# Second layer's first products as seven products of quarters for two column groups by two token halves

## The chip, the core and the metric

One core of one Trainium2 chip runs the whole program. The metric is the device time of one execution in microseconds (us). TensorE (PE) multiplies, ScalarE (ACT), VectorE (DVE) and GpSimd (POOL) do the elementwise work, and SyncE (SP) issues nearly all transfers.

## What is computed

A thresholded attention gives 2304 tokens of 512 numbers; a gated layer and a second layer follow. The change is in the second layer alone (fp32 throughout, d_model 512, d_ff 2048):

```python
x = _moe_ref(x=x, **moe_kwargs)          # gate, val, out: 512 -> 1536 -> 512
return _moe2_ref(x=x, **moe2_kwargs)
...
def _moe2_ref(x, w_in, w_out):
    h = x @ w_in                          # 2304 x 2048, "the first products"
    g = np.where(h >= 1, h, np.where(h <= -1, 0.0, (h + 1) ** 2 / 4))
    return g @ w_out                      # 2304 x 512
```

## The kernel before

Every fp32 product is made of three fp32r matmuls: both factors are split into a high part (an ACT copy that rounds) and a low part (a DVE subtraction), and high·high, high·low and low·high are added up in PSUM. The attention runs first (about 0 to 300 us), then the gated layer (called layer 0, to 747.5 us), then the second layer. Tokens go in three passes of 768 (`T`), each in two halves of 384 (`HT`); d_ff goes in column groups of 128 (`f`), 12 in layer 0 and 16 in the second. x lies transposed, so that a matmul has 128 columns of weights as its stationary side and 384 tokens as its moving side.

`order` lists the steps: layer, pass, column group. One step of the second layer is a call of `hidden` (L497): for each half, `up` (L466) makes 4 blocks of 128 of the contraction by 3 matmuls of 384 (L472 to L474, into a PSUM tile `pu`); then DVE clamps (L522), ACT squares (L525), DVE takes the maximum with h (L526), ACT rounds it to `hh` (L529) and DVE leaves the rest in `hl` (L531). Between these stand the splits of the next group's weights (`split_parts`, L183 and L185: `ih`, `il` for the first products, `oh`, `ol` for the second) and, in the last step of a pass, the splits of the next pass's x (`split_xs`, L462 and L464). Behind the step, PE gets the second products of the step before it (`down`, L546): 6 blocks of 128 tokens by 3 matmuls of 512 (L563, into PSUM tiles `w`), which add up over a pass. After a pass `finish` (L568) moves its six blocks out of PSUM, in turn on DVE (L586) and ACT (L588), and sends them off. Layer 0 is alike; its `finish` writes `xall`, the x of the second layer, with pieces of 512 and 256 (L573, L575).

So PE's order in the second layer is: 24 matmuls of 384, 18 of 512, and so on, 48 times. Each engine works in the order in which the program wrote its instructions; an instruction that waits holds all behind it. PE has two PSUM banks of first products (`a0`, `a1`) and three double ones of second products.

Of the kernel before, what the change touches and what calls it, by code (L numbers as in the profile page):

```python
# [29 lines left out]
def kernel(  # L30
# [17 lines left out]
    nc = tc.nc  # L48
# [21 lines left out]
    raw = ctx.enter_context(pool("raw", 2))  # L70
    zero = ctx.enter_context(pool("zero", 1, space=DRAM))
    scratch = ctx.enter_context(pool("scratch", 1, space=DRAM))
    ws0 = ctx.enter_context(pool("ws0", 1))
# [9 lines left out]
    rbs = [const.tile([P, S], F32, name=f"rb_{i}") for i in range(2)]  # L83
# [6 lines left out]
    xflat = const.tile([P, 2 * KD * T], F32R, name="xflat")  # L90

# [19 lines left out]
    def load_w(ph, g):  # L111

        f, i = divmod(g, 3 - ph)
        ins, wo = ((w_gate, w_val), w_out) if ph == 0 else ((w2_in,), w2_out)
        if i < len(ins):
            src = ins[i][:, 2 * f * P : 2 * (f + 1) * P].rearrange("(k p) f -> p k f", p=P)
        else:
            src = wo[f * P : (f + 1) * P, :].rearrange("p (k f) -> p k f", k=KD)
        early = ph == 0 and g < 6
        t = (raw if early else pools["words"]).tile([P, 2 * KD * P], F32, tag="raw", name="raw")  # L120
# [44 lines left out]
    def split_list(ph, t, f, whole=True):  # L165

        ni = 2 - ph
        m = len(wsp_n)
        wsp_n.append(f)
        a, b = (ws0 if m % x == 0 else pools[y] for x, y in ((2, "ws"), (3, "wo")))  # L170
        ih = a.tile([P, 2, KD, P], F32R, tag="ih", name="ih")
        il = a.tile([P, 2, KD, P], F32R, tag="il", name="il")
        oh = b.tile([P, DM], F32R, tag="oh", name="oh")
        ol = b.tile([P, DM], F32R, tag="ol", name="ol")
# [12 lines left out]

        return [part(*x) for x in at]
# [4 lines left out]
    def attention():  # L193
# [141 lines left out]
        def spread(p):  # L335
            dr = drs.pop(p)
            for a, n, o in ((nf * P, nf * P, 0), (R, R, 2 * nf * P)):
                src = bass.AP(tensor=dr.tensor, offset=dr.offset + o, ap=[[a, 2], [0, D], [1, n]])
                nc.sync.dma_start(out=rbs[p % 2][:, (o > 0) * nf * P :][:, :n], in_=src)

        def normalise(p, s):
            x, c = x_of(p), slice(s * HS, s * HS + HS)
            nc.gpsimd.tensor_tensor(x[:, c], x[:, c], rbs[p % 2][:, c], op=ALU.mult)
# [105 lines left out]
    def ffn(att):  # L449


        with ExitStack() as st:
            sb = lambda n, b, **kw: st.enter_context(pool(n, b, reuse_waits="tile", **kw))
# [43 lines left out]
            def hidden(ph, t, f, nxt, work):  # L497


                hh = hs.tile([P, T], F32R, tag="hh", name="hh")  # L500
                hl_ = hs.tile([P, T], F32R, tag="hl", name="hl")
                sp = split_parts(*nxt) if nxt and nxt not in wsp else iter(())
                xs = iter(())
                for n in range(2):
                    c = slice(n * HT, n * HT + HT)
                    act = hp_.tile([P, HT], F32, tag="act", name="act")
                    if ph == 0:
                        if (s := (ph, t, f, n)) in early:
                            pg, pv = early.pop(s)
                            nc.scalar.activation(act, pg, AF.Sigmoid)  # L510
                        else:
                            pg, pv = (ps_a.tile([P, 512], F32, tag=f"a{i}", name="pgv")[:, :HT] for i in range(2))
                            up(0, t, f, n, 0, pg)
                            nc.scalar.activation(act, pg, AF.Sigmoid)  # L514
                            up(0, t, f, n, 1, pv)
                        if n == 0:
                            run(itertools.islice(sp, 1))
                        nc.vector.tensor_tensor(act, pv, act, op=ALU.mult)  # L518
                    else:
                        pu = ps_a.tile([P, 512], F32, tag=f"a{n}", name="pu")[:, :HT]  # L520
                        up(1, t, f, n, 0, pu)
                        nc.vector.tensor_scalar(act, pu, -1.0, 1.0, op0=ALU.max, op1=ALU.min)  # L522
                        if n == 1:
                            run(itertools.islice(xs, 4))
                        nc.scalar.activation(act, act, AF.Square, scale=0.5, bias=half)  # L525
                        nc.vector.tensor_tensor(act, pu, act, op=ALU.max)  # L526
                        if n == 1:
                            run(itertools.islice(xs, 4))
# [9 lines left out]
                hts[ph, t, f] = (hh, hl_)  # L538
# [7 lines left out]
            def down(ph, t, f, y, blocks=range(T // P)):  # L546
                hh, hl_ = hts[ph, t, f]
                oh, ol = wsp[ph, t, f][2:]
                first, last = f == 0, f == NF[ph] - 1
                if ph == 0:  # L550
                    for a, b, d in spans:
                        ds_, c = slice(d * P, d * P + P), slice(a - d * T, b - d * T)
                        new = first and a % 512 == 0
                        for m, (l, r) in enumerate(((oh, hh), (oh, hl_), (ol, hh))):
                            nc.tensor.matmul(  # L555
                                at(y, a, b), l[:, ds_], r[:, c], start=new and m == 0, stop=last and m == 2,
                                skip_group_check=True,
                            )
                    return
                for i in blocks:  # L560
                    ts_ = slice(i * P, i * P + P)
                    for m, (l, r) in enumerate(((hh, oh), (hl_, oh), (hh, ol))):
                        nc.tensor.matmul(  # L563
                            y[i % 3][:, i // 3], l[:, ts_], r,
                            start=first and m == 0, stop=last and m == 2,
                        )
# [24 lines left out]
            order = [(ph, t, f) for ph in range(2) for t in range(NPASS) for f in range(NF[ph])]  # L591
# [13 lines left out]
            early, taken = {}, []  # L605
# [3 lines left out]
            for step, free in att:  # L609
# [4 lines left out]
                if free:  # L614
                    pools["words"] = sb("words", 6)
# [3 lines left out]
                    pools["ws"] = sb("ws", 1)  # L619
                    pools["wo"] = sb("wo", 2)  # L620
                    hp_ = sb("hp_", 2)
# [11 lines left out]
            hs = sb("hs", 2, side="right")  # L633
            ps_a = sb("ps_a", 1, space=PSUM)
            for i in range(2):
                highs[i] = kp.tile([P, 3 * KD * P], F32, name=f"high_{i}")
            ring[:0] = [kp.tile([P, 3 * KD * P], F32, name=f"w32_{i + 2}") for i in range(3)]
            w2s = [kp.tile([P, 2 * KD * P], F32, name=f"w2_{i}") for i in range(2)]
# [5 lines left out]
            for s in range(len(order)):  # L644
                nxt = order[s + 1] if s + 1 < len(order) else None
                t = order[s][:2]
                ops = 8 if t == (0, 0) else 5
                if s + 2 < len(order) and order[s + 2][:2] > (0, 0):
                    load_step(*order[s + 2])
                hidden(*order[s], nxt, itertools.islice(conv, ops))  # L650
                if s > 0:
                    ph, t, f = order[s - 1]
                    if f == 0:
                        y = [wide() for _ in range(3)]
                    if s < len(order) - 1:
                        down(ph, t, f, y)
                        if f == NF[ph] - 1:
                            finish(ph, t, y)

            for b in (range(3), (3,), (4,), (5,)):  # L660
                down(*order[-2], y, b)
                for i in b:
                    down(*order[-1], y, (i,))
                    finish(ph, t, y, (i,))
# [50 lines left out]
```

## Time and profile before

| | |
|---|---|
| median of 3 runs | 1160.7 us (1160.56 to 1160.76) |
| the profiled execution | 1160.46 us |
| span in its profile | 1158.7 us |
| PE busy | 1131.9 us, 98% of the span, 6516 matmuls |
| DVE busy | 796.9 us, 69% |
| ACT busy | 559.5 us, 48% |
| POOL busy | 137.6 us, 12%, all of it before 310 us |

The span is what the engines' records cover; 1.8 us of the profiled execution lie around it. In the timeline an entry has its start, its length, engine, line and operation, and in brackets how long its engine had been idle before it and what ended that. Busy shares are means over stages; what a change in one stage is worth is read in that stage.

### The profile page before, as it was taken

The numbers are of one execution on the slowest core, as the hardware profiler recorded it, in microseconds if no ns is written. First come the engines' busy times: TensorE is split into PE (matmuls) and PEld (weight loads), VectorE is DVE, ScalarE is ACT, GpSimd is POOL, SyncE is SP. The second block draws the span as 40 slices with busy tenths as digits, with TensorE's granted clock in tenths as the row PEclk, the third lists the DMA queues.
The fourth block names the chain that finished last, engine by engine and source line by source line (L and its number), as shares of the span: only waits on it lengthen the run. The fifth ranks groups of instructions, "written<-read, shape, count | busy, mean of one in ns | idle before, by whom it ended". The sixth has DMA issues, their size and how long they took to land.

```text
span 1158.7 us, 17531 instructions
## 1 busy us (share of the span) xinstructions
PE 1131.9 (98%) x6516; PEld 968.6 (84%) x6516; DVE 796.9 (69%) x1491; ACT 559.5 (48%) x1027; POOL 137.6 (12%) x315
## 2 busy tenths in 40 slices
PE   8999999999899999999999999999999999999998
PEld 5655655556799999999999999999898989989897
DVE  6888888887699998665676662465557555575554
ACT  5777777787344444333343332443435343454333
POOL 3444544554100000000000000000000000000000
PEclk9999999999899999999999999999999999999999
DMA  4323223221645655434434323121211412041201
GB/s 129 87 74 101 69 74 83 67 58 33 244 165 198 208 194 193 162 136 161 168 129 163 136 88 131 37 72 56 63 47 57 145 55 73 19 163 56 72 2 55
DMA packets 59381, 122.33 MB, mean 106 GB/s; under 512 B 8976, under 2 KB 35232, under 8 KB 59296
## 3 DMA queue, kind: packets, MB, share of 16 engines
q1 hardware_dynamic: 59152, 121.20, 32.1%
q8 instruction: 52, 0.85, 0.3%
q14 instruction: 33, 0.27, 0.1%
q10 hardware_dynamic: 144, 0.00, 0.0%
HBM read 98.57 MB, written 22.62 MB: 105 GB/s over the span
## 4 chain that ended last, share of the span: by engine, by line
PE 90%; DVE 6%; issue 2%; ACT 2%; DMA 1%; POOL 0%; DVEq 0%; ACTq 0%; POOLq 0%
PE w L563 17%; PE w L555 13%; PE pgv L472 8%; PE pgv L473 8%; PE pgv L474 8%; PE av L312 6%; PE pu L474 6%; PE pu L473 6%; PE pu L472 6%; PE w L288 5%; PE w L245 5%; DVE s L254 2%; PE w L241 2%; DVE p L274 1%; DVE high L158 1%
## 5 line engine op out<-in xcount | busy, mean ns | idle before, releaser
L472 PE MATMUL pgv<-xflat,ih 128*128 128x384 f32 x560 | 188.6, 337 | 6.0 <-ACT act L514 4.1
L473 PE MATMUL pgv<-xflat,ih 128*128 128x384 f32 x560 | 188.4, 336 | 0.0
L474 PE MATMUL pgv<-xflat,il 128*128 128x384 f32 x560 | 188.2, 336 | 0.0
L529 ACT ACTIVATE hh<-act 128x384 fp32r<-128x384 f32 x168 | 88.5, 527 | 180.8 <-DVE act L518 119.0
L525 ACT ACTIVATE act<-act,half 128x384 f32<-128x384 f32 x96 | 59.2, 617 | 167.7 <-DVE act L522 167.7
L531 DVE TENSOR_TENSOR hl<-act,hh 128x384 fp32r<-128x384 f32 x168 | 93.5, 557 | 62.0 <-ACT hh L529 62.0
L254 DVE TENSOR_SCALAR_CACHE_REDUCE s<-w,nscale 128x576 f32<-128x576 f32 x144 | 112.7, 816 | 33.7 <-PE w L245 23.9
L474 PE MATMUL pu<-xflat,il 128*128 128x384 f32 x384 | 128.9, 336 | 0.0
L473 PE MATMUL pu<-xflat,ih 128*128 128x384 f32 x384 | 128.9, 336 | 0.0
L472 PE MATMUL pu<-xflat,ih 128*128 128x384 f32 x384 | 128.4, 334 | 0.0
L518 DVE TENSOR_TENSOR act<-pgv,act 128x384 f32<-128x384 f32 x70 | 38.9, 555 | 118.9 <-PE pgv L474 115.1
L563 PE MATMUL w<-oh,hh 128*128 128x512 f32 x288 | 113.9, 395 | 0.4 <-DVE xall L586 0.4
L563 PE MATMUL w<-ol,hh 128*128 128x512 f32 x288 | 114.0, 396 | 0.0
L563 PE MATMUL w<-oh,hl 128*128 128x512 f32 x288 | 113.9, 396 | 0.0
L472 PEld LDWEIGHTS pgv<-xflat,ih 128*128 128x128 f32 x560 | 105.9, 189 | 8.4 <-ACT act L514 4.7
L274 DVE SCALAR_TENSOR_TENSOR p<-s,mx,ex 128x576 f32<-128x576 f32 x144 | 112.0, 810 | 0.5 <-POOL lt L281 0.5
L266 ACT ACTIVATE ex<-s,mx 128x576 f32<-128x576 f32 x144 | 104.8, 775 | 7.1 <-DVE s L254 6.7
L473 PEld LDWEIGHTS pgv<-xflat,ih 128*128 128x128 f32 x560 | 105.9, 189 | 1.8 <-DVE xflat L464 0.2
L474 PEld LDWEIGHTS pgv<-xflat,il 128*128 128x128 f32 x560 | 106.0, 189 | 0.0
L526 DVE TENSOR_TENSOR act<-pu,act 128x384 f32<-128x384 f32 x96 | 53.5, 558 | 70.2 <-ACT act L525 70.2
L514 ACT ACTIVATE act<-pgv 128x384 f32<-128x384 f32 x70 | 34.2, 489 | 134.6 <-PE pgv L474 134.4
L288 PEld LDWEIGHTS w<-ident,p 128*128 128x128 f32 x576 | 62.8, 141 | 41.6 <-ACT ex L266 36.6
(82 smaller groups left out, 2184.4 us busy)
## 6 DMA issues: line engine op xcount, KB each, us to landing
w<-saved SPq DMA_DIRECT2D x48, 512.0 KB
w<-saved SPq DMA_DIRECT2D x24, 768.0 KB
raw<-in_moe_w_out_dram SPq DMA_DIRECT2D x28, 512.0 KB
saved<-w SPq DMA_DIRECT2D x12, 768.0 KB
raw<-in_moe_w_in_dram SPq DMA_DIRECT2D x16, 512.0 KB
saved<-w SPq DMA_DIRECT2D x16, 512.0 KB
raw<-in_moe_w_gate_dram SPq DMA_DIRECT2D x12, 512.0 KB
raw<-in_moe_w_val_dram SPq DMA_DIRECT2D x12, 512.0 KB
```

The costliest lines, as they stand in the source:

```text
L254: nc.vector.tensor_scalar(t[:, e], w[:, :, :HS], nscale, None, op0=ALU.mult, op1=ALU.min, accum_out=mx[:, 0, e : e + 1])
L266: nc.scalar.activation(ex[:, e], t[:, e], AF.Exp, scale=-1.0, bias=mx[:, 0, e : e + 1])
L274: nc.vector.scalar_tensor_tensor(pr[:, e], t[:, e].rearrange("p a b -> p (a b)"), mx[:, 1, e : e + 1], ex[:, e].rearrange("p a b -> p (a b ...
L288: nc.tensor.transpose(wt[:, e, cs], pr[:, e, cs], ident)
L312: nc.tensor.matmul(av[e * D : e * D + D, :n], vs[p % 3][:, e, c], rt[r][:, e, c] if c < nf else rl[r], start=c == 0, stop=c == nf,)
L472: nc.tensor.matmul(ps, ih[:, i, kk], xh[:, kk, c], start=(kk == 0), stop=False)
L473: nc.tensor.matmul(ps, ih[:, i, kk], xl[:, kk, c], start=False, stop=False)
L474: nc.tensor.matmul(ps, il[:, i, kk], xh[:, kk, c], start=False, stop=(kk == KD - 1))
L529: nc.scalar.activation(hh[:, c], act, AF.Copy)
L531: nc.vector.tensor_tensor(hl_[:, c], act, f32(hh[:, c]), op=ALU.subtract)
L555: nc.tensor.matmul(at(y, a, b), l[:, ds_], r[:, c], start=new and m == 0, stop=last and m == 2, skip_group_check=True,)
L563: nc.tensor.matmul(y[i % 3][:, i // 3], l[:, ts_], r, start=first and m == 0, stop=last and m == 2,)
```

## The change

Two neighbouring column groups form a pair `q` (8 to a pass, 24 in all). A pair's first products are a 2 by 2 matrix of quarters: two column groups by two token halves, with the contraction of 512 cut in two halves as well. Instead of eight products of quarters, seven are made (P.0 to P.6), each 2 blocks of the contraction by 3 matmuls of 384; their factors are quarters of x and of the weights, or sums and differences of such quarters, and the four results are put together from the seven by additions. POOL makes the factors: `w_sums` four subtractions of 256 columns a pair, `x_sums` four additions of 768 columns a pass. `x_splits` splits seven blocks of 768 columns a pass, `w_splits` 512, 256 and 1024 columns a pair, `out_split` the weights of the second products. Then PE makes the 36 matmuls of 512 of the pair before. The activation works on 768 columns of one group: ReLU and square on ACT, one operation on DVE, the copy `hh` on ACT, `hl` on DVE. There are still two PSUM banks, `ps[0]` and `ps[1]`; P.2 adds to what P.0 left in `ps[0]`. SBUF is laid out anew, with the order of instructions in attention and layer 0 kept on every engine.

```diff
-                    else:
-                        pu = ps_a.tile([P, 512], F32, tag=f"a{n}", name="pu")[:, :HT]
-                        up(1, t, f, n, 0, pu)
-                        nc.vector.tensor_scalar(act, pu, -1.0, 1.0, op0=ALU.max, op1=ALU.min)
...
-                        nc.scalar.activation(act, act, AF.Square, scale=0.5, bias=half)
-                        nc.vector.tensor_tensor(act, pu, act, op=ALU.max)
...
+            PRODUCTS = ((0, 0, 0, 1), (1, 1, 1, 1), (0, 2, 3, 0), (1, 3, 4, 1), (0, 4, 5, 1), (1, 5, 6, 0), (0, 6, 2, 0))
...
+                op = nc.gpsimd.tensor_tensor
+                op(s1, a21, a22, op=ALU.add)
+                op(s2, s1, a11, op=ALU.subtract)
+                op(s4, a12, s2, op=ALU.subtract)
+                op(a21, a11, a21, op=ALU.subtract)
+                xops[t] = (a11, a12, s2, a21, s1, a22, s4)
...
+            def x_splits(t):
+                for i, a in enumerate(xops.pop(t)):
+                    xh, xl = (x.rearrange("p (k t) -> p k t", k=HK) for x in x_block(i))
+                    nc.scalar.activation(xh, a, AF.Copy)
+                    nc.vector.tensor_tensor(xl, a, f32(xh), op=ALU.subtract)
+                    yield
...
+                for o, a, b in ((t1, b12, b11), (t2, b22, t1), (t3, b22, b12), (t4, b21, t2)):
+                    nc.gpsimd.tensor_tensor(o, a, b, op=ALU.subtract)
...
+            def activate(i, c, h):
+
+                r = sqs[:, i]
+                nc.scalar.activation(r, c, AF.Relu, scale=0.5, bias=half)
+                nc.scalar.activation(r, r, AF.Square)
+                yield
+                nc.vector.scalar_tensor_tensor(c, c, 1.0, r, op0=ALU.max, op1=ALU.min)
+                nc.scalar.activation(h[0], c, AF.Copy)
+                yield
+                nc.vector.tensor_tensor(h[1], c, f32(h[0]), op=ALU.subtract)
+                yield
+
+            def pair(q):
...
+                if q + 1 < NPASS * NQ:
+                    w_sums(q + 1)
+                if j == NQ - 2 and t + 1 < NPASS:
+                    x_sums(t + 1)
+                outs = [lambda i=i: out_split(q, i) for i in range(2)]
+                xs = x_rest.pop(t, None) if j == 0 else None
+                product(0, ps)
+                nc.scalar.activation(s1, ps[0], AF.Copy)
+                if xs:
+                    run(itertools.islice(xs, 2))
+                product(1, ps)
+                add(c[0][:, t0], ps[1], s1)
+                if xs:
+                    run(xs)
+                else:
+                    while outs:
+                        outs.pop(0)()
+                product(2, ps)
+                nc.scalar.activation(u2, ps[0], AF.Copy)
+                product(3, ps)
+                add(u3, ps[1], u2)
+                product(4, ps)
+                add(c[1][:, t1], ps[0], u3)
+                product(5, ps)
+                add(c[0][:, t1], ps[1], u2)
+                product(6, ps)
+                add(c[1][:, t0], ps[0], u2)
...
+            def behind(q, outs, acts):
...
+                if j == NQ - 1 and t + 1 < NPASS:
+                    xs = x_splits(t + 1)
+                    do(2)
+                    run(itertools.islice(xs, 2))
+                    do(4)
+                    run(itertools.islice(xs, 2))
+                    run(acts[0])
+                    x_rest[t + 1] = xs
+                    return acts[1:]
+                a, b = acts[-2:]
+                for x in acts[:-2]:
+                    run(x)
+                next(a)
+                do(1)
+                next(a)
+                do(2)
+                run(a)
+                do(3)
+                for o in outs:
+                    o()
+                run(b)
+                return []
...
+            for q in range(NPASS * NQ):
+                outs, acts = pair(q)
...
+                left = behind(q, outs, left + acts)
...
+                if q == 0:
+                    down(*order[-1][1:], y)
+                    finish(0, NPASS - 1, y)
+                else:
...
+                        down_pair(q - 1, y)
+                        if q % NQ == 0:
+                            finish(1, q // NQ - 1, y)
```

Three places show what this makes of the engines' queues. The first is ACT at the end of the second layer's first pass, around the evictions of that pass. `w_118` to `w_123` are the PSUM tiles of the second products, `w_2` to `w_4` and `w_0` in other rows buffers of loaded weights, and what stands in brackets is the engine that a row waits for. Before:

```order
L525 ACTIVATE act<-act,half 128x384 [waits DVE_49,Activation_49]
L529 ACTIVATE hh<-act 128x384 [waits DVE_49]
L588 ACTIVATE xall<-w_122 128x512 [waits PE_49]
L588 ACTIVATE xall<-w_123 128x512 [waits DVE_49]
L588 ACTIVATE xall<-w_121 128x2x256 [waits DVE_49]
L525 ACTIVATE act<-act,half 128x384 [waits DVE_49,Activation_49]
L529 ACTIVATE hh<-act 128x384 [waits DVE_49]
```

Now, behind the first pair of the second pass up to the copy of P.0 in the pair after it (L645, whose input `pu` is the bank that P.2 wants):

```order
L623 ACTIVATE hh<-vals 128x768 [waits DVE_49]
L585 ACTIVATE win_88<-w_0_82 128x256 [waits DMAHW4_49,PE_49]
L585 ACTIVATE win_88<-tsum 128x1024 [waits Pool_49]
L596 ACTIVATE wout_89<-w_2_3098 128x512
L596 ACTIVATE wout_3005<-w_3_3099 128x512
L619 ACTIVATE sqs<-vals,half 128x768
L620 ACTIVATE sqs<-sqs 128x768 [waits Activation_49]
L623 ACTIVATE hh<-vals 128x768 [waits DVE_49]
L746 ACTIVATE xall<-w_119 128x512 [waits PE_49]
L746 ACTIVATE xall<-w_120 128x512 [waits DVE_49]
L746 ACTIVATE xall<-w_118 128x2x256 [waits DVE_49]
L645 ACTIVATE act<-pu 128x384 [waits PE_49]
```

The three evictions (L588, now L746) have moved from behind one step's short activation to behind the weight splits and the second activation of a pair, and the first row that takes a first product out of PSUM stands behind them.

The second place is DVE at the start of a pass, where `pu` is again a first product and `xmore` and `xflat` hold the split x. Before, the x splits stand between a half's activation steps:

```order
L464 TENSOR_TENSOR xflat<-xall,xflat 128x384 [waits Activation_49] x4
L522 TENSOR_SCALAR act<-pu 128x384 [waits PE_49]
L464 TENSOR_TENSOR xflat<-xall,xflat 128x384 [waits Activation_49] x2
L526 TENSOR_TENSOR act<-pu,act 128x384 [waits Activation_49]
L464 TENSOR_TENSOR xflat<-xall,xflat 128x384 [waits Activation_49] x2
L531 TENSOR_TENSOR hl<-act,hh 128x384 [waits Activation_49]
```

Now:

```order
L625 TENSOR_TENSOR hl<-vals,hh 128x768 [waits Activation_49]
L568 TENSOR_TENSOR xflat<-ssum,xflat 128x768 [waits Activation_49]
L568 TENSOR_TENSOR xflat<-xall,xflat 128x768 [waits Activation_49]
L636 TENSOR_TENSOR vals<-pu,act 128x384 [waits DVE_49,PE_49]
L568 TENSOR_TENSOR xflat<-raw_86,xflat 128x768 [waits Activation_49]
L636 TENSOR_TENSOR high_84<-pu,act 128x384 [waits PE_49,Activation_49]
L636 TENSOR_TENSOR vals<-pu,high_84 128x384 [waits DVE_49,PE_49]
L636 TENSOR_TENSOR vals<-pu,act 128x384 [waits PE_49] x2
```

The low parts of blocks 4 and 5 now stand ahead of the addition (L636) that takes P.1 out of its bank, and block 6 behind it.

The third is PE in that pair, from the first matmul of P.2 to the first of P.4; `win_88` holds the high and `win_3004` the low parts of the weights. There is nothing like it before, where a half's 12 matmuls ran into a bank of their own:

```order
L611 MATMUL pu<-xmore,win_88 128x384 [waits Activation_49]
L611 MATMUL pu<-xmore,win_88 128x384 [waits DVE_49]
L611 MATMUL pu<-xmore,win_3004 128x384
L611 MATMUL pu<-xmore,win_88 128x384 x2
L611 MATMUL pu<-xmore,win_3004 128x384
L611 MATMUL pu<-xflat,win_88 128x384 [waits DVE_49]
L611 MATMUL pu<-xflat,win_88 128x384
L611 MATMUL pu<-xflat,win_3004 128x384
L611 MATMUL pu<-xflat,win_88 128x384 x2
L611 MATMUL pu<-xflat,win_3004 128x384
L611 MATMUL pu<-xflat,win_88 128x384 [waits Activation_49]
```

P.2 waits for an ACT instruction (the copy of P.0), P.3 for a DVE one (the addition that frees P.1's bank), and P.4 for an ACT one again.

## Rows read from the trace of the kernel before

**Rows 1.** Windows, second layer; busy us of PE, PEld, DVE, ACT, POOL, sums, clock, DMA.

```profile
762.00:876.00 114.00, 114.00 (x574) 102.92 (x573) 62.54 (x111) 45.44 (x82) 0.00 (x0) 1.00 0.18 56
```

**Rows 2.** Timeline of PE, one column group; start us, us, operation, what it waited for.

```profile
772.63 0.33 PE L472 MATMUL pu<-xflat,ih 128*128 128x384 f32 x1
...
776.82 0.39 PE L563 MATMUL w<-oh,hh 128*128 128x512 f32 x1
...
781.01 0.33 PE L472 MATMUL pu<-xflat,ih 128*128 128x384 f32 x1
```

**Rows 3.** Groups by line and form, all; busy us, mean ns of one, idle before.

```profile
L183 ACT ACTIVATE oh<-w 128x512 fp32r<-128x512 f32 x84 | 51.8, 616 | 0.0
...
L183 ACT ACTIVATE ih<-w 128x1024 fp32r<-128x1024 f32 x34 | 35.9, 1056 | 14.7 <-DVE w L162 14.7
...
L514 ACT ACTIVATE act<-pgv 128x384 f32<-128x384 f32 x70 | 34.2, 489 | 134.6 <-PE pgv L474 134.4
...
L303 ACT ACTIVATE r<-w 128x256 f32<-128x256 f32 x32 | 12.1, 378 | 20.2 <-PE w L288 20.2
...
L586 DVE COPY xall<-w 128x512 f32<-128x512 f32 x9 | 5.7, 683 | 2.6 <-PE w L563 2.6
...
L343 POOL TENSOR_TENSOR xall<-xall,rb 128x288 f32<-128x288 f32 x32 | 26.5, 829 | 19.8 <-ACT high L138 16.3 <-DMA rb<-dr 2.3
...
L464 DVE TENSOR_TENSOR xflat<-xall,xflat 128x768 fp32r<-128x768 f32 x4 | 3.6, 954 | 0.0
...
L462 ACT ACTIVATE xflat<-xall 128x768 fp32r<-128x768 f32 x4 | 3.2, 855 | 0.0
```

**Rows 4.** Timeline of all engines, from a product's end to its hidden value.

```profile
774.56 0.33 PE L474 MATMUL pu<-xflat,il 128*128 128x384 f32 x1
...
774.93 0.56 DVE L522 TENSOR_SCALAR act<-pu 128x384 f32<-128x384 f32 x1 [1.04 <-PE pu L474]
...
775.59 0.62 ACT L525 ACTIVATE act<-act,half 128x384 f32<-128x384 f32 x1 [2.28 <-DVE act L522]
...
776.24 0.56 DVE L526 TENSOR_TENSOR act<-pu,act 128x384 f32<-128x384 f32 x1 [0.75 <-ACT act L525]
...
776.89 0.53 ACT L529 ACTIVATE hh<-act 128x384 fp32r<-128x384 f32 x1 [0.69 <-DVE act L526]
...
777.32 0.62 ACT L183 ACTIVATE ih<-w 128x512 fp32r<-128x512 f32 x1
```

**Rows 5.** Timeline of DVE and ACT, evictions of the first pass's output.

```profile
892.05 1.88 DVE L586 COPY xall<-w 128x512 f32<-128x512 f32 x3
...
892.77 1.20 ACT L588 ACTIVATE xall<-w 128x512 f32<-128x512 f32 x2 [0.74 <-DVE xall L586]
```

**Rows 6.** Timeline of PE at its end.

```profile
1150.46 0.50 PE L563 MATMUL w<-oh,hh 128*128 128x512 f32 x1 [0.41 <-DVE xall L586]
```

**Rows 7.** Timeline, PE around its two idle stretches of the switch from attention.

```profile
307.65 0.69 PE L472 MATMUL pgv<-xflat,ih 128*128 128x384 f32 x1 [3.70 <-ACT act L514]
...
310.65 0.34 PE L472 MATMUL pgv<-xflat,ih 128*128 128x384 f32 x1
...
313.31 0.44 PE L472 MATMUL pgv<-xflat,ih 128*128 128x384 f32 x1 [1.97 <-DVE act L518]
...
317.53 0.39 PE L555 MATMUL w<-hh,ol 128*128 128x512 f32 x1
```

**Rows 8.** Windows just behind those two stretches; columns as in Rows 1.

```profile
308.00:310.00 2.00, 2.00 (x7) 2.00 (x7) 1.97 (x3) 0.00 (x0) 1.24 (x1) 0.50 0.13 52
...
314.00:316.00 2.00, 2.00 (x8) 2.00 (x7) 2.00 (x3) 1.19 (x3) 0.00 (x0) 0.50 1.03 323
```

**Rows 9.** Timeline, POOL and DVE together; then DVE's same operation alone.

```profile
306.68 2.56 POOL L343 TENSOR_TENSOR xall<-xall,rb 128x288 f32<-128x288 f32 x2 [16.34 <-ACT high L138]
307.03 1.55 DVE L154 TENSOR_SCALAR high<-w 128x1536 uint32<-128x1536 uint32 x1
...
370.53 0.95 DVE L154 TENSOR_SCALAR high<-w 128x1536 uint32<-128x1536 uint32 x1
```

More of the change, by code (lines that the diff above doesn't have):

```diff
@@ L82 @@
     xall = const.tile([P, KD, NT], F32, name="xall")
[L83 removed]
+    rbs = const.tile([P, 2 * S], F32, name="rb")
     corners = [const.tile([P, P], F32, name=f"corner_{i}") for i in range(2)]
@@ new lines, in out_split, with load_pair, product @@
+            def out_split(q, i):
+                src = w32[q][i][:, KD * P : 2 * KD * P]
+                oh, ol = wout(q, i)
+                nc.scalar.activation(oh, src, AF.Copy)
+                nc.vector.tensor_tensor(ol, src, f32(oh), op=ALU.subtract)
+            def load_pair(q):
+                f = 2 * (q % NQ)
+                w32[q] = [turn(), turn()]
+                for i in range(2):
+                    nc.sync.dma_start(out=w32[q][i][:, : 2 * KD * P], in_=saved[1, f + i])
+            def product(i, ps):
+                bank, xi, wi, new = PRODUCTS[i]
+                xh, xl = (x.rearrange("p (k t) -> p k t", k=HK) for x in x_block(xi))
+                wh, wl = (w[:, wi * HC : (wi + 1) * HC].rearrange("p (k f) -> p k f", k=HK) for w in wins)
+                for k in range(HK):
+                    for m, (l, r) in enumerate(((wh, xh), (wh, xl), (wl, xh))):
+                        nc.tensor.matmul(
+                            ps[bank], l[:, k], r[:, k], start=bool(new) and k == m == 0,
+                            stop=k == HK - 1 and m == 2, skip_group_check=True,
+                        )
@@ new lines, in down_pair @@
+            def down_pair(q, y, blocks=range(T // P)):
+                for i in range(2):
+                    (hh, hl_), (oh, ol) = hts[q][i], wout(q, i)
+                    first, last = q % NQ == i == 0, q % NQ == NQ - 1 and i == 1
+                    for b in blocks:
+                        ts_ = slice(b * P, b * P + P)
+                        for m, (l, r) in enumerate(((hh, oh), (hl_, oh), (hh, ol))):
+                            nc.tensor.matmul(
+                                y[b % 3][:, b // 3], l[:, ts_], r, start=first and m == 0, stop=last and m == 2
+                            )
@@ L544, in at, with down @@
                 return y[a // 1024].rearrange("p a b -> p (a b)")[:, a % 1024 : a % 1024 + b - a]
[L546 to L562, printed above, removed]
+            def down(t, f, y):
+                hh, hl_ = hts[0, t, f]
+                oh, ol = wsp[0, t, f][2:]
+                first, last = f == 0, f == NF[0] - 1
+                for a, b, d in spans:
+                    ds_, c = slice(d * P, d * P + P), slice(a - d * T, b - d * T)
+                    new = first and a % 512 == 0
+                    for m, (l, r) in enumerate(((oh, hh), (oh, hl_), (ol, hh))):
                         nc.tensor.matmul(
-                            y[i % 3][:, i // 3], l[:, ts_], r,
-                            start=first and m == 0, stop=last and m == 2,
+                            at(y, a, b), l[:, ds_], r[:, c], start=new and m == 0, stop=last and m == 2,
+                            skip_group_check=True,
                         )
@@ L651, in ffn @@
                 if s > 0:
-                    ph, t, f = order[s - 1]
                     if f == 0:
                         y = [wide() for _ in range(3)]
[L655 to L661, printed above, removed]
+                    down(t, f, y)
+                    if f == NF[0] - 1:
+                        finish(0, t, y)
@@ L662, in ffn @@
+            for b in (range(4), (4,), (5,)):
+                down_pair(q - 1, y, b)
                 for i in b:
-                    down(*order[-1], y, (i,))
-                    finish(ph, t, y, (i,))
+                    down_pair(q, y, (i,))
+                    finish(1, NPASS - 1, y, (i,))
     with tc.manual_schedule():
```

173 lines of the change are left out of this document (127 added, 46 removed).

## The prediction

> **What bounds the kernel now.** The page's shares (table above) put PE at 98%; since a share is a mean over stages, the windows come next: in a stretch of the second layer PE is busy 114.00 of 114.00 us, DVE 62.54, ACT 45.44, POOL none [rows 1]. PE's timeline prices its work: 24 matmuls of 384 run from 772.63 to 776.82, 4.19 us or 0.1746 each, and 18 of 512 from there to 781.01, 4.19 or 0.2328 each [rows 2]. So the second layer is as long as its matmuls. Fewer of them save their time only while operands and free PSUM banks keep coming; the groups by line and the timeline price what ACT and DVE do for that [rows 3, 4].
>
> **What goes.** 48 x 24 = 1152 matmuls of 384 become 24 x 42 = 1008; 144 x 0.1746 = **25.1 us** off PE. The second products stay (864 of 512), as does PE's order ahead of the layer.
>
> **What the new order asks of ACT and DVE.** Durations, in columns: ACT copy 256 .38, 384 .53, 512 .62, 768 .855, 1024 1.06; 384 out of PSUM .49 [rows 3, 4]. An ACT operation with a bias takes .62 where the copy of its size takes .53, so ReLU with bias on 768 is .95. DVE: 768 .954, 384 .56, eviction of 512 .683 [rows 3, 4], of 256 by ACT's ratio .43. ACT's eviction of 512 is .60, and DVE's three in a row overlap by .08 each (1.88 against 3 x .683) [rows 5]. ACT starts its next operation .10 before the last ends; handing over costs .04 PE to DVE, .10 DVE to ACT, .03 ACT to DVE [rows 4], and about .06 to PE, my estimate between those. Times below count from the end of P.6.
>
> *Ordinary pair (20 of 24).* PE has 36 x 0.2328 = 8.38 of second products, then P.0 (6 x 0.1746 = 1.05) and P.1 (1.05) before P.2 needs `s1` (L645). ACT has, one after the other, two activations (each ReLU .95, square .855, `hh` .855), the weight splits (.62, .38, 1.06) and two waits for DVE's part of the activation; it is free at 8.50. P.0's last matmul is issued out at 9.43, and DVE took up a product .20 after that point (774.56 + .17 to 774.93 [rows 4]), so `s1` cannot start before 9.63. ACT has 1.1 to spare, and PE's place for P.2, a product later, some 1.5. No wait, cost nothing; this spare is the cover, and what exceeds it comes straight onto PE.
>
> *First pair of a pass (3).* There is no activation to await, but x blocks 4 and 5 stand in both queues. After P.0: `s1` .20 to .69; the two copies to 1.45 and 2.21; the low parts (L568) 1.48 to 2.43 and 2.35 to 3.30; only then the addition that frees P.1's bank, 3.21 to 3.77. P.3 starts at 3.83 where PE would be there at 2.09: 1.7 each, **5.1**.
>
> *Second pair of passes 2 and 3 (2).* The first activation there is the one held back from the pass before: its `hh` runs 1.84 to 2.70, behind DVE's .80 to 1.75. Then ACT has the first new group's ReLU (2.60), square, `hh` (to 6.38), the weight splits (to 7.62), the two `out_split` copies (to 8.66), the second group's ReLU (8.56), square and `hh` (11.48 to 12.34, behind DVE's 10.44 to 11.39), and behind all this the evictions. These alternate: an ACT eviction waits for a DVE one (0.74 at 892.77 [rows 5]). DVE's first is held by the last `hl` (12.37 to 13.32): 13.24 to 13.92, ACT's 14.01 to 14.61 and 14.61 to 15.21, `s1` 15.11 to 15.60, P.2 at 15.66. PE is there at 8.38 + 2.09 = 10.47: 5.2 each, **10.4**.
>
> *Switch from layer 0 (pair 1).* Only 18 matmuls of layer 0 stand ahead (4.19), so PE is at P.2 at 6.28. ACT and DVE have the same two activations (`hl` to 10.52), then nine pieces of 512 and 256 in turn, to 13.83; `s1` ends at 14.22, P.2 starts at 14.28: **8.0**.
>
> *End.* The last group's `hh` ends at 7.26 and `hl` at 8.24, the 27 matmuls in front at 6.28: waits of 1.0 and .75, against .41 now [rows 6]: **+1.4**.
>
> Waits 5.1 + 10.4 + 8.0 + 1.4 = 24.9 against 25.1: **-0.2** before two things that this trace shows only ahead of the layer.
>
> *Clock.* After PE had stood 3.70 us its granted clock was 0.50, the 1.2 GHz level; 9 matmuls then took 3.0 (307.65 to 310.65) instead of 1.57. After 1.97 idle it was 0.50 again; 12 of 384 and 2 of 512 took 4.22 (313.31 to 317.53) instead of 2.56 [rows 7, 8]. So 1.4 and 1.7 lost. The three new waits over 5 us lie above both; I charge the lower price, **+4.2**. The waits of 1.7 lie just under the shorter stretch and follow a busy PE, so I take nothing for them. Bounds: none loses (0), all six lose 1.7 (10.2).
>
> *POOL.* Its 32 instructions of 288 columns took .83 on average, 2.9 ns a column [rows 3], so .74 for 256 and 2.2 for 768. Where two overlapped a DVE operation, that took 1.55 in place of .95, a hold of .6 [rows 9]. `w_sums` has four per pair, at the pair's start. Their holds strike ACT's chain only if they reach the low parts and `hl`; an ordinary pair has spare. In the two pairs with `x_sums` POOL works 4 x 2.2 + 4 x .74 = 11.8 us, and there holds of some 2 us against a spare of .5 leave 1.5 each: **+3.0**, bounds 0 and 7.
>
> **Sum.** -0.2 + 4.2 + 3.0 = +7.0 on the profiled 1160.46, so 1167.5; the median 1160.7 lies .24 above that execution: **1167.7**. The forecast's own range, with one term at a bound, is 1163.5 to 1173.
>
> **Rivals.**
>
> *The evictions do not alternate, and it is faster.* If DVE and ACT empty the banks side by side at the two pass ends and at the switch, ACT begins with them right behind its `hh` and not behind DVE's. Then `s1` ends at 14.2 in a second pair, a wait of 3.9 instead of 5.2, and at 11.6 at the switch, 5.3 instead of 8.0. Waits 5.1 + 2 x 3.9 + 5.3 + 1.4 = 19.6; less 25.1 that is -5.5, so 1155.2, with clock and POOL free. Against it: the order rows show ACT's evictions waiting for DVE, and so does the trace [rows 5]. It decides once waits and losses together stay under 22.8 (25.1 less 2.3). Chance .10.
>
> *Waits as summed, but the clock stays up and POOL hides.* -0.2: 1160.5. For: the two stretches with the low clock follow a time of scattered matmuls, and the new waits a busy layer. Chance .14.
>
> *All waits are hidden,* for in that stretch DVE is idle for 45% and ACT for 60% [rows 1]: 1160.7 - 25.1 = 1135.6. Against it stand the order rows, whose queues are serial. Chance .04.
>
> *POOL slows every ordinary pair.* `w_sums` runs against DVE's additions and low parts. Three of four holds of .6 on the chain are 1.8 against a spare of 1.5: .3 x 20 = 6 more, 1173.7; all four .9 x 20 = 18, some 1186. Against: DVE's additions wait for PE anyway. Chance .12.
> In the Trainium skill, page "SBUF — State Buffer", section "Who interferes with whom", with the locks spelled out in "SBUF: two separate sides", a DVE operation with two SBUF inputs and a GpSimd operation that reads SBUF take one port pair in turn, and the loser is blocked for the whole instruction of the other. The 1.55 against .95 agrees that POOL can hold DVE, though there DVE's operation had one input, and the hold was .6 and not a whole .83; an operation with two inputs beside POOL's stands in no row used here. By that rule each hold would be .74, three of them 2.2 against 1.5, .7 x 20 = 14 more, some 1182.
>
> **How the numbers follow.** Forecast .60, the rivals .10, .14, .04 and .12. About 0.2% (2.3 us) is what a measurement here can tell from no change, so "same" is 1158.4 to 1163.0: the clock-free rival, .14. Faster: .10 + .04 = .14. Slower: .60 + .12 = .72. For 8 in 10 I take the forecast (.60), the clock-free rival (.14) and the nearer half of POOL's (.06), to 1173.7 and 3 us above it, half of the forecast's other bounds: **1159 to 1177**.
>
> **What would show it.** Right: 144 matmuls fewer on PE (6372 less what the records miss), 1008 of them into `pu`; PE's timeline with idle of about 8 us before P.2 of pair 1, 5 before P.2 of pairs 9 and 17, released by ACT's copy (L645), and 1.7 before P.3 of pairs 0, 8 and 16, released by the addition (L636); windows behind the long waits with the clock at 0.50. Wrong: idle of PE in ordinary pairs, POOL named as the releaser of DVE there, long waits with the clock at 1.00, or ACT evicting while DVE does. The likeliest errors are the pass ends and the switch, each the end of a queue of some fifteen operations, and the clock.

## The result and the profile after

The changed kernel takes 1171.85 us (median of 4 runs, 1171.38 to 1172.31) where the kernel before took 1160.63 beside it: 11.2 us more, ratio 1.0099 with a 95% interval of 1.0082 to 1.0117. Forecast were 1167.7 us, slower with .72, and a range of 1159 to 1177. The profiled execution took 1171.48 us, against 1160.46 of the one that the sum was made on.

The page of the changed kernel, its span and busy times, and of part 2 PE's busy tenths and its granted clock in 40 slices:

```profile
span 1169.7 us, 17320 instructions
...
PE 1117.0 (95%) x6372; PEld 951.9 (81%) x6372; DVE 842.4 (72%) x1440; ACT 619.3 (53%) x1048; POOL 262.5 (22%) x423
...
PE   8999999999899999999999999979998999979998
...
PEclk9999999999899999999999999989999899989999
```

PE makes 6372 matmuls, the 144 fewer that the change promised. Behind the middle, at some 770, 900 and 1040 us, slices have less PE and a lower clock. The view of waits says what PE waited for there; its columns are total us, times, and the longest:

```profile
PE pu L611 <- ACT act L645: 16.8, 3, 7.5
...
PE pu L611 <- DVE vals L636: 5.5, 3, 2.4
...
PE pu L611 <- DVE high L636: 3.4, 2, 1.7
...
PE w L703 <- ACT hh L623: 0.6, 1, 0.6
...
PE w L703 <- DVE hl L625: 0.5, 1, 0.5
```

The same view of the kernel before, from 740 us to the end, has one line, the wait at the end [rows 6]:

```profile
PE w L563 <- DVE xall L586: 0.4, 1, 0.4
```

So none of the other waits was there before. Of the ten waits now, three are for the copy of P.0, three for the addition behind P.1, two for the addition behind P.3 in the pairs with `x_sums`, two at the end. PE's timeline at the switch shows what stands behind a wait too:

```profile
747.46 3.29 PE L611 MATMUL pu<-xmore,win 128*128 128x384 f32 x18
753.13 6.02 PE L611 MATMUL pu<-xflat,win 128*128 128x384 f32 x24 [2.38 <-DVE vals L636]
758.99 0.39 PE L721 MATMUL w<-hh,wout 128*128 128x512 f32 x1
...
763.18 2.25 PE L611 MATMUL pu<-xmore,win 128*128 128x384 f32 x12
772.90 2.29 PE L611 MATMUL pu<-xmore,win 128*128 128x384 f32 x6 [7.47 <-ACT act L645]
...
780.38 0.39 PE L703 MATMUL w<-wout,hh 128*128 128x512 f32 x1
```

The second layer starts at 747.46 as before (747.5), so the whole difference lies in it. 24 matmuls from 753.13 to 758.99 take 5.86 us where 24 took 4.19 before [rows 2], and 30 from 772.90 take 7.48 for 5.24. The windows there have the granted clock in the last column but two:

```profile
752.00:756.00 4.00, 2.87 (x11) 2.87 (x12) 2.57 (x4) 0.00 (x0) 2.60 (x2) 0.72 0.00 0
...
772.00:776.00 4.00, 3.10 (x10) 3.10 (x11) 1.81 (x3) 2.38 (x5) 0.34 (x1) 0.50 0.20 29
...
788.00:792.00 4.00, 4.00 (x24) 3.82 (x23) 2.05 (x3) 2.38 (x4) 2.67 (x3) 1.00 0.00 0
```

The bill, by starts of matmuls (a wait by starts is .16 longer than the idle shown, since a matmul's shown end lies that far past the next one's start): matmuls -25.1; P.3 of pairs 0, 8, 16 +2.5 + 1.7 + 1.7; P.2 of pair 1 +7.6; P.2 of pairs 9 and 17 +4.8 each; P.5 of pairs 6 and 14 +1.8 each; the end +.9; half clock +1.7, +2.2, +2.4 and +2.4 behind the waits of pairs 0, 1, 9 and 17. These terms add up to +11.2, and the two profiled executions differ by 11.0.

Where the long waits come from is seen in the timeline of ACT and DVE at the end of the first pass, around pair 9:

```profile
905.12 0.84 ACT L623 ACTIVATE hh<-vals 128x768 fp32r<-128x768 f32 x1 [1.02 <-DVE vals L622]
905.87 0.58 ACT L746 ACTIVATE xall<-w 128x512 f32<-128x512 f32 x1
906.00 0.96 DVE L625 TENSOR_TENSOR hl<-vals,hh 128x768 fp32r<-128x768 f32 x1 [0.91 <-ACT hh L623]
906.87 1.88 DVE L744 COPY xall<-w 128x512 f32<-128x512 f32 x3
...
907.59 1.20 ACT L746 ACTIVATE xall<-w 128x512 f32<-128x512 f32 x2 [1.14 <-DVE xall L744]
...
908.68 0.49 ACT L645 ACTIVATE act<-pu 128x384 f32<-128x384 f32 x1
...
909.22 2.29 PE L611 MATMUL pu<-xmore,win 128*128 128x384 f32 x6 [4.66 <-ACT act L645]
```

P.0 had been made by 903.6 (its six matmuls start at 902.32). Its copy (L645) stands behind the second group's `hh` and three evictions, and two of those wait 1.14 us for DVE, which is at `hl` first.

### The profile page after: what moved, and what is told of

It is laid out like the page before. It is cut to its first block, busy times and chain, and to the rows that moved or that the text cites. A ratio compares the mean times of both kernels' runs of the same rounds, so it can differ in the third digit from the quotient of the medians.

```text
span 1169.7 us, 17320 instructions
## 1 busy us (share of the span) xinstructions
PE 1117.0 (95%) x6372; PEld 951.9 (81%) x6372; DVE 842.4 (72%) x1440; ACT 619.3 (53%) x1048; POOL 262.5 (22%) x423
## 4 chain that ended last, share of the span: by engine, by line
PE 84%; DVE 8%; ACT 4%; issue 3%; DMA 1%; POOL 0%; DVEq 0%; POOLq 0%; ACTq 0%
PE w L703 15%; PE pu L611 14%; PE w L721 12%; PE pgv L480 8%; PE pgv L481 8%; PE pgv L482 8%; PE av L317 6%; PE w L293 5%; PE w L250 5%; DVE s L259 2%; PE w L246 1%; DVE p L279 1%; DVE high L163 1%; ACT sqs L619 1%; ACT sqs L620 1%
## 5 line engine op out<-in xcount | busy, mean ns | idle before, releaser
L480 PE MATMUL pgv<-xflat,win 128*128 128x384 f32 x560 | 189.1, 338 | 5.6 <-ACT act L520 4.1
L481 PE MATMUL pgv<-xflat,win 128*128 128x384 f32 x560 | 188.7, 337 | 0.0
L482 PE MATMUL pgv<-xflat,win 128*128 128x384 f32 x560 | 188.5, 337 | 0.0
L703 PE MATMUL w<-wout,hh 128*128 128x512 f32 x576 | 184.3, 394 | 0.6 <-ACT hh L623 0.6
L721 PE MATMUL w<-hh,wout 128*128 128x512 f32 (+1 forms) x576 | 146.5, 336 | 0.0
L703 PEld LDWEIGHTS w<-wout,hh 128*128 128x128 f32 x576 | 108.2, 188 | 25.5 <-ACT hh L623 1.0
L611 PE MATMUL pu<-xflat,win 128*128 128x384 f32 x576 | 110.9, 349 | 8.9 <-DVE vals L636 5.5
L611 PEld LDWEIGHTS pu<-xflat,win 128*128 128x128 f32 x576 | 106.5, 198 | 10.5 <-DVE vals L636 6.5
L703 PE MATMUL w<-wout,hl 128*128 128x512 f32 x288 | 113.7, 395 | 0.5 <-DVE hl L625 0.5
L480 PEld LDWEIGHTS pgv<-xflat,win 128*128 128x128 f32 x560 | 106.2, 190 | 8.2 <-ACT act L520 4.8
L481 PEld LDWEIGHTS pgv<-xflat,win 128*128 128x128 f32 x560 | 106.3, 190 | 1.8 <-DVE xflat L472 0.2
L721 PEld LDWEIGHTS w<-hh,wout 128*128 128x128 f32 x576 | 98.0, 188 | 11.3
L482 PEld LDWEIGHTS pgv<-xflat,win 128*128 128x128 f32 x560 | 106.3, 190 | 0.0
L721 PE MATMUL w<-hl,wout 128*128 128x512 f32 (+1 forms) x288 | 97.1, 337 | 0.0
```

Source lines behind the costliest of these rows:

```text
L480: nc.tensor.matmul(ps, ih[:, i, kk], xh[:, kk, c], start=(kk == 0), stop=False)
L481: nc.tensor.matmul(ps, ih[:, i, kk], xl[:, kk, c], start=False, stop=False)
L482: nc.tensor.matmul(ps, il[:, i, kk], xh[:, kk, c], start=False, stop=(kk == KD - 1))
L611: nc.tensor.matmul(ps[bank], l[:, k], r[:, k], start=bool(new) and k == m == 0, stop=k == HK - 1 and m == 2, skip_group_check=True,)
L703: nc.tensor.matmul(y[b % 3][:, b // 3], l[:, ts_], r, start=first and m == 0, stop=last and m == 2)
L721: nc.tensor.matmul(at(y, a, b), l[:, ds_], r[:, c], start=new and m == 0, stop=last and m == 2, skip_group_check=True,)
```

## The experiments

The theory: the seven products cost what their matmuls cost, and the loss is waits of PE on serial queues, each removable by moving the operation in front of the one that PE waits for, plus the clock. Rivals: one chain stands behind all waits, so that one removed returns at the next product; POOL holds whatever DVE does; each wait costs its own half clock. Differences are to the runs of the kernel before that were made beside each kernel; the change stands at +11.2.

**The low parts behind the addition** (`e1_add_first`).

```diff
                 nc.scalar.activation(s1, ps[0], AF.Copy)
-                if xs:
-                    run(itertools.islice(xs, 2))
                 product(1, ps)
                 add(c[0][:, t0], ps[1], s1)
```

> The change with one edit: in the first pair of a pass, x blocks 4 to 6 are split behind the addition that frees P.1's bank. Queue theory: the waits before P.3 of pairs 0, 8 and 16, which are 2.5, 1.7 and 1.7 us from due to start, fall to 0.4 or less, and the half clock behind the first (1.67 us lost) goes too: 1171.9 - 4.7 - 1.7, some 1165.5 us. Rival (the low parts themselves are late): PE waits at P.4 or P.5 instead for about as long, 1169 to 1172 us.

Measured: 1167.96 us against 1159.98 (ratio 1.0074, 1.0059 to 1.0089), +8.0. No wait before P.3 is left, and the half clock at pair 0 is gone. The time is 2.5 us above the expected 1165.5, though, and the rival has that part: PE stands before P.5, .34 in pairs 8 and 16 and 1.35 in pair 0 (2.5 together by starts). In pair 0 POOL makes the weight sums of pair 1 at that time:

```profile
750.82 0.95 DVE L568 TENSOR_TENSOR xflat<-ssum,xflat 128x768 fp32r<-128x768 f32 x1
751.02 1.35 POOL L577 TENSOR_TENSOR tsum<-w,tsum 128x256 f32<-128x256 f32 x1
...
751.69 1.50 DVE L568 TENSOR_TENSOR xflat<-xall,xflat 128x768 fp32r<-128x768 f32 x1
...
752.33 1.44 POOL L577 TENSOR_TENSOR tsum<-w 128x256 f32<-128x256 f32 x1
```

Where they meet, DVE's operation takes 1.5 us in place of .95 and POOL's 1.4 in place of .74, as if they took turns: POOL's ends at 752.37, .60 after DVE's first, and DVE's second at 753.19, .82 after that.

**The same, with POOL's sums for pair 1 made later** (`e6_late_w_sums`).

```diff
                 add(u3, ps[1], u2)
+                if q == 0:
+                    nc.gpsimd.tensor_copy(dummy, u3[:, :1])
+                    w_sums(1)
```

(The call at the start of pair 0 is taken out; the small copy makes POOL wait for the addition.)

> The run with the low parts behind the addition, with one more edit: POOL makes the weight sums for pair 1 only when the addition after P.3 of pair 0 is done, not beside the low parts of blocks 4 to 6. If the 1.4 us of idle left before P.5 of pair 0 came from POOL holding those low parts (1.5 us each in place of 0.95), it falls to about 0.3 us as in pairs 8 and 16, and the low parts take 0.95 again; else it stays at 1.4 us. One run, 1166 to 1168 us either way.

Measured: one run, 1166.81 us against 1160.14. The idle before P.5 of pair 0 is .28, and the same low parts take .95:

```profile
752.12 0.95 DVE L568 TENSOR_TENSOR xflat<-xall,xflat 128x768 fp32r<-128x768 f32 x1
752.99 0.95 DVE L568 TENSOR_TENSOR xflat<-raw,xflat 128x768 fp32r<-128x768 f32 x1
```

So POOL held them. It fits the change itself, where the first of the three pass starts cost 2.5 and the other two 1.7: there the two low parts ahead of the addition run in pair 0 beside the same weight sums:

```profile
750.02 1.19 DVE L568 TENSOR_TENSOR xflat<-ssum,xflat 128x768 fp32r<-128x768 f32 x1 [0.22 <-ACT xflat L567]
...
751.14 1.47 DVE L568 TENSOR_TENSOR xflat<-xall,xflat 128x768 fp32r<-128x768 f32 x1
```

Together they take .76 more than twice .95; in pair 8, with no weight sums beside them, they take .96 and .95.

**Late evictions** (`e2_late_evictions`). At the switch and at pass ends `finish` is not called; its pieces go to the next pair:

```diff
...
+                ev = iter(evict)
+                go = lambda n: [e() for e in itertools.islice(ev, n)]
+                go(max(len(evict) - 6, 0))
                 add(u3, ps[1], u2)
+                go(2)
                 product(4, ps)
                 add(c[1][:, t1], ps[0], u3)
+                go(2)
                 product(5, ps)
                 add(c[0][:, t1], ps[1], u2)
+                go(2)
```

> The change with one edit: the evictions at the switch and at two pass ends are issued in the next pair, spread behind its additions of P.3, P.4 and P.5, not ahead of its copy of P.0. Queue theory: the copy then follows ACT's hh of the second group: waits before P.2 of pair 1 from 7.6 to about 3.4, of pairs 9 and 17 from 4.8 to about 2.0; 9.8 less, 1162 us if the clock still falls at all three, 1157.5 if it stays up after 2.0. Rival (the evictions are late next: they hold the additions, or the second products wait for their banks): the waits turn up at P.5, P.6 or the first 512-column matmuls, 1168 to 1172 us.

Measured: 1158.12 us (10 runs) against 1159.98 (ratio .9986, .9976 to .9995), -1.9, so 13.1 us off the change; no new wait of PE over .15 shows.

```profile
769.30 2.29 PE L611 MATMUL pu<-xmore,win 128*128 128x384 f32 x6 [3.31 <-ACT act L645]
...
777.39 0.39 PE L709 MATMUL w<-wout,hh 128*128 128x512 f32 x1
...
903.46 1.31 PE L611 MATMUL pu<-xmore,win 128*128 128x384 f32 x6 [1.83 <-ACT act L645]
...
909.10 0.39 PE L709 MATMUL w<-wout,hh 128*128 128x512 f32 x1
```

The waits are as expected (7.5 to 3.3 and 4.7 to 1.8 of idle). The 30 matmuls behind 3.31 took 8.09 and lost 2.9 us; those behind 1.83 took at most 5.64 and lost .4, with the clock at 1.00: the better of the two expected cases.

**Evictions by tile, in their place** (`e5_evict_by_tile`). It makes the mechanism of the prediction's first rival true. In the change an ACT eviction waits for a DVE one that reads the same PSUM tile; with no tile shared between the two engines there is no such wait.

```diff
-                        if (i + a if end else i) % 2 == 0:
+                        if i % 3 == 1 if t < NPASS - 1 else (i + a if end else i) % 2 == 0:
```

(and in the pieces of layer 0's last pass, by `a // 1024 == 1`.)

> The change with one edit: at the switch and at the two pass ends the evictions go to an engine by the PSUM tile they read (the middle tile to DVE, the other two to ACT), not in turn, so that no ACT eviction waits for a DVE one; their place in the queues stays. This is the first rival's mechanism, made true. Theory: the copy of P.0 comes 0.8 us earlier in pairs 9 and 17 (wait 4.8 to 3.9) and 2 us earlier in pair 1 (7.6 to 5.4), with the clock falling as before: 1171.9 - 3.6, some 1168 us. Against it: if ACT's own pieces are as long as the turns were, no gain, 1171 to 1172.5 us.

Measured: 1166.53 us against 1160.14 (ratio 1.0050, 1.0033 to 1.0067), +6.4; the four runs spread from 1164.5 to 1168.6. The idle is 5.38 before P.2 of pair 1 and 3.78 in pairs 9 and 17, 5.5 and 3.9 by starts, where the rival was worked out with 5.3 and 3.9:

```profile
903.49 0.84 ACT L623 ACTIVATE hh<-vals 128x768 fp32r<-128x768 f32 x1 [1.03 <-DVE vals L622]
904.24 2.04 ACT L746 ACTIVATE xall<-w 128x512 f32<-128x512 f32 x4
...
906.14 0.51 ACT L645 ACTIVATE act<-pu 128x384 f32<-128x384 f32 x1
...
906.71 2.29 PE L611 MATMUL pu<-xmore,win 128*128 128x384 f32 x6 [3.78 <-ACT act L645]
```

Had the evictions not alternated in the change, it would still have been slower: the clock falls either way.

**Late out splits beside the x sums** (`e3_out_splits_late`). The change's timeline in pair 6, POOL and DVE:

```profile
853.40 1.89 POOL L558 TENSOR_TENSOR ssum<-xall 128x768 f32<-128x768 f32 x1
853.91 0.56 DVE L636 TENSOR_TENSOR vals<-pu,act 128x384 f32<-128x384 f32 x1 [1.06 <-ACT wout L596]
854.38 3.70 DVE L597 TENSOR_TENSOR wout<-w,wout 128x512 fp32r<-128x512 f32 x2
...
855.37 2.17 POOL L559 TENSOR_TENSOR ssum<-ssum,xall 128x768 f32<-128x768 f32 x1
...
858.01 0.55 DVE L636 TENSOR_TENSOR high<-pu,act 128x384 f32<-128x384 f32 x1
858.61 2.36 PE L611 MATMUL pu<-xflat,win 128*128 128x384 f32 x12 [1.68 <-DVE high L636]
```

The two out splits (L597) take 3.70 us, elsewhere 1.29, and the addition that P.5 waits for stands behind them. The edit:

```diff
-                else:
+                elif j != NQ - 2:
                     while outs:
                         outs.pop(0)()
...
                 add(c[1][:, t0], ps[0], u2)
+                if j == NQ - 2:
+                    while outs:
+                        outs.pop(0)()
```

> The change with one edit: in the two pairs in which POOL makes the x sums, the out weight splits are issued behind the last addition, not ahead of the one after P.3; POOL does the same work at the same time. If POOL holds only those DVE operations that have two SBUF operands, the additions (one operand in PSUM) pass, the wait of 1.8 us before P.5 of pairs 6 and 14 goes, and the splits find POOL nearly done: 1171.9 - 3.7, some 1168.2 us. Rival (POOL holds whatever DVE does): the additions are held in place of the splits, 1171 to 1172.5 us.

Measured: 1167.23 us against 1159.98 (ratio 1.0063, 1.0046 to 1.0080), +7.3, 3.9 less than the change. PE does not wait in pairs 6 and 14 any more, though POOL works at the same time:

```profile
855.33 1.87 POOL L559 TENSOR_TENSOR ssum<-ssum,xall 128x768 f32<-128x768 f32 x1
855.98 0.56 DVE L636 TENSOR_TENSOR high<-pu,act 128x384 f32<-128x384 f32 x1 [1.53 <-PE pu L611]
856.95 0.56 DVE L636 TENSOR_TENSOR vals<-pu,high 128x384 f32<-128x384 f32 x1 [0.41 <-PE pu L611]
```

An addition with one operand in PSUM takes .56 beside POOL as alone; POOL's own operation takes 1.87 there and 2.17 beside the splits.

**What a wait costs in clock** (`e4_clock_probe`). Idle copies on ACT, of 256 to 1024 columns, ahead of the copy of P.0 in six ordinary pairs; they compute nothing that is used.

```diff
                 product(0, ps)
+                for n in PROBE.get(q, ()):
+                    nc.scalar.activation(early_raw[1][:, :n], rbs[:, :n], AF.Copy)
                 nc.scalar.activation(s1, ps[0], AF.Copy)
```

> The change with idle copies on ACT ahead of the copy of P.0 in six ordinary pairs, so that PE waits before P.2: about 1.0 (pair 3), 1.5 (5), 2.0 (11), 2.3 (13), 2.5 (19) and 3.4 us (21). It prices the clock: the five products behind a wait take 5.24 us at full clock. If it falls only after waits longer than the 1.8 us that did no harm in the change, the first two lose nothing, the last two 1.7 to 2.2 each, and the middle two tell where it begins. Rival (each wait costs its own half clock): a loss that grows from pair 3 on. Time 1171.9 + 12.7 of waits + 3 to 8 of clock, 1188 to 1193 us.

Measured: one run, 1192.29 us. PE's timeline behind three of the waits, and windows at the first and the third:

```profile
947.25 1.31 PE L611 MATMUL pu<-xmore,win 128*128 128x384 f32 x6 [2.13 <-ACT act L649]
...
981.49 2.29 PE L611 MATMUL pu<-xmore,win 128*128 128x384 f32 x6 [2.57 <-ACT act L649]
...
1129.09 2.29 PE L611 MATMUL pu<-xmore,win 128*128 128x384 f32 x6 [3.65 <-ACT act L649]
```

```profile
947.00:951.00 4.00, 3.75 (x21) 3.75 (x22) 2.68 (x5) 1.74 (x4) 0.00 (x0) 1.00 0.34 98
...
1130.00:1134.00 4.00, 4.00 (x14) 4.00 (x13) 1.44 (x3) 0.56 (x2) 0.00 (x0) 0.50 0.44 135
```

The 30 matmuls behind a wait, start of the first to start of what follows, less 5.24:

| idle before P.2, us | 1.03 | 1.46 | 2.13 | 2.57 | 2.80 | 3.65 |
|---|---|---|---|---|---|---|
| lost behind it, us | .10 | .13 | .11 | 1.44 | 2.82 | 2.59 |

Where the clock stays at 1.00 this reckoning gives .10 to .13. The loss does not grow with the wait; it is there or not, and the last two lost more than the 1.7 to 2.2 expected. Each point is one stretch of one execution, so the other runs count: behind 1.35 to 1.68 nothing; behind 1.83, in four stretches, three times .35 to .40 at a clock of 1.00 and once 1.68 (in the kernel that follows); behind 2.38 or 2.39 1.67 in four kernels and nothing in one (this one); behind 3.3 and more always 1.5 to 2.9. The rival of a gradual price falls.

**The first, the late evictions and the late out splits in one kernel** (`c1_combined`), by the three diffs above.

> The three single edits together (low parts behind the addition, late evictions, late out splits). If they are separate waits, their gains over the change add up: 3.9 + 13.7 + 4.6, so 1171.9 - 22.2, some 1149.7 us, with about 3.3 us of idle left before P.2 of pair 1, 1.8 before P.2 of pairs 9 and 17, 1.4 at P.5 of pair 0 and 1.1 at the end. Rival (one chain stands behind all of them, so that a wait removed returns at the next product): 1153 us or more.

Measured: 1151.38 us against 1160.51 (ratio .9921, .9905 to .9938), -9.1. By what the single runs gained beside their own runs of before (3.2, 13.1 and 3.9 off +11.2) it should be -9.0. (The expected 1149.7 was added up from the medians themselves; the runs of before beside them lie up to .65 apart.) The idle left is as expected, 1.36 at P.5 of pair 0, 3.29 and twice 1.83 before P.2, and 1.1 at the end, with .34 more before P.5 of pairs 8 and 16. The gains add up; the rival of one chain falls.

**The queues put in order** (`c2_best`). Its core, in the pair behind a first pair: the first pair's second activation (`tail`) and the evictions, all on ACT now, follow the copy of P.0:

```diff
                 nc.scalar.activation(s1, ps[0], AF.Copy)
+                if tail and q == 1:
+                    next(tail)
+                go(2 if q == 1 else 3)
                 product(1, ps)
...
                 nc.scalar.activation(u2, ps[0], AF.Copy)
+                if q == 1:
+                    go(6)
+                if tail:
+                    next(tail)
                 product(3, ps)
                 add(u3, ps[1], u2)
...
+                if tail and q > 1:
+                    run(tail)
                 product(4, ps)
                 add(c[1][:, t1], ps[0], u3)
+                go(6)
```

> All of that, and the rest of the queue theory: in the first pair of a pass the second group's activation runs on into the next pair, behind the copy of P.0; the late evictions are ACT's alone; the out splits of a first pair stand behind its additions; POOL's weight sums for pair 1 wait for the addition after P.3 of pair 0; x block 6 is split behind that addition; the end makes five of the last but one pair's blocks ahead. If queue order is all that kept the seven products from paying, what is left is the 25.1 us of matmuls less about 0.3 us for each pass start, 0.5 to 1 at the end and 1 elsewhere: 1160.3 - 25.1 + 2.5, some 1138 us, 1136 to 1140. Rival (ACT and DVE have no room for it: the moved operations hold the additions of pairs 1, 9 and 17, 1.5 us or more in each): 1141 to 1147 us.

Measured: 1139.00 us (4 runs, 1138.38 to 1139.20) against 1160.51; ratio .9813, .9798 to .9827. That is 21.5 us under the kernel before, of the 25.1 that the matmuls give, where the change stands 11.2 over it with the same matmuls. The window over nearly all of the second layer, and one of the two longest waits left in it, before P.6 of pair 9:

```profile
747.00:1133.00 386.00, 384.50 (x1902) 341.45 (x1901) 268.62 (x358) 235.71 (x350) 109.55 (x101) 1.00 0.20 70
```

```profile
893.95 1.31 PE L611 MATMUL pu<-xflat,win 128*128 128x384 f32 x6 [0.33 <-DVE vals L637]
```

PE is busy 384.50 of 386.00 us at a clock of 1.00.

## Why the prediction was right, and where not

- **Matmuls, -25.1.** Right: 144 fewer, each at its old price.
- **Ordinary pair, 0.** Right: PE does not wait in any of them but pairs 6 and 14, which are under POOL. Their spare is real: in pair 3 the probe put 2.7 us of copies (1.04, 1.06 and .63) in front of the copy of P.0 and got 1.03 of idle, 1.2 by starts, so the spare is the 1.5 that I gave for PE's place. I counted 20 such pairs; there are 18 (24 less three, two and the one at the switch), so the POOL rival's .3, .7 and .9 a pair come to 5, 13 and 16, not 6, 14 and 18.
- **Pass starts, 5.1.** Measured 6.0. The term has the right cause (the low parts ahead of the addition) and misses one effect: POOL held the low parts in pair 0, for .8 more. I had charged POOL only to the pairs with `x_sums`.
- **Second pairs, 10.4; switch, 8.0.** Measured 9.6 and 7.6. The queue, summed row by row, was .4 too long each time. (I wrote nine pieces at the switch; there are eight, and the sum had eight.)
- **End, +1.4.** Measured +.9.
- **POOL, +3.0.** Measured 3.7, in the two pairs named and by a hold on DVE as said, but not where I looked for it: I let the holds reach ACT's chain through the low parts and `hl`, against a spare of .5 that no row gives; what was held is the two out splits, with the addition that P.5 waits for behind them. The Trainium skill, page "SBUF — State Buffer", section "Who interferes with whom" (the locks stand in "SBUF: two separate sides"), lets a DVE operation with two SBUF inputs and a GpSimd operation that reads SBUF exclude each other for a whole instruction. The runs agree: the pair of splits grew by 2.41 us (3.70 for 1.29) beside two operations of POOL of 1.89 and 2.17, and ends .54 after the second of them (858.08 and 857.54), while additions with a PSUM operand kept .56. What I worked out of it for ordinary pairs (some 1182) did not come, since there two operations of DVE are held by .20 and .24 (1.16 and 1.20 for .96), which lies under the spare.
- **Clock, +4.2: the step that failed, by its size.** Measured 8.6. I took the lower of two prices, 1.4 a wait, from 9 matmuls behind one idle stretch [rows 7]; the three long waits cost 2.2, 2.4 and 2.4, and the wait of 2.4 us at pair 0, which I had put among the short ones at 1.7 and charged nothing, cost 1.7. Only 9 matmuls ran slowly behind that stretch; behind each of the three long waits 14 or 15 did. The difference of 4.4 accounts for the forecast's error of 4.2. The bound of 10.2 held it (with it the sum is 1173.7, where I wrote 1173).

So the sign was right for the reason given. The waits came to 27.9 as forecast (24.9 and POOL's 3.0); that the sums agree so closely is luck, since single terms were off by up to .9 each way. Of the rivals, that all waits are hidden is wrong for this order of the queues, and nearly right (21.5 of the 25.1) for another, as the last kernel shows: there was room on ACT and DVE all the time.

## What to carry to other kernels

Count a saving of matmuls only after summing, row by row, the queue in front of the first operation that frees a PSUM bank, above all where two stages meet (a pass end, a layer switch): here 32.7 us (11.2 over and 21.5 under the kernel before) lay between two arrangements of ACT's and DVE's work around the same matmuls. Put the copy that PE waits for ahead of work that has later due times. A wait that brings the clock down costs 1.4 to 2.9 us more than its length here, so take the longest waits away first, and keep GpSimd's two-input work away from DVE operations with both inputs in SBUF where these stand in front of PE.

## What the runs showed of the hardware that was not expected

The price of the clock does not grow with the wait: in the probe nothing is lost behind idle of up to 2.13 us, and 1.4 to 2.8 us from 2.57 on. Between, it goes either way: 2.4 us cost 1.67 in four kernels and nothing in one, and 1.83 us cost 1.68 once in four. What decides there was not tried. The same idle of 4.66 us cost between 1.5 and 2.8 us from place to place and run to run; some kernels with such waits spread more too (1164.5 to 1168.6 in one, against 1138.4 to 1139.2 for the last kernel), but the change, which has all three, kept within 1171.4 to 1172.3. And DVE and POOL hold each other in both directions: DVE's low part took 1.5 for .95, POOL's sum 1.4 for .74.
